# A recurrence and an MLP in one kernel: one gate tile of its own, the last token in its unit's tile, two groups of matmuls at other places

## The chip, the cores and the metric

The kernel runs on one core of a Trainium2 chip. The time is device microseconds of an execution; the number compared is the median of several executions. A profile records one execution: TensorE's matmuls (PE) and weight loads (PEld), VectorE (DVE), ScalarE (ACT), GpSimd (POOL) and the queue that issues transfers (SP). Each engine works off its own queue in order and waits on semaphores for what other engines make.

## The reference

Inputs q, k, v and f_logit have 4 batches, 8 heads, 768 tokens and 48 elements per head. A linear recurrence with a gate runs along the tokens, and its result goes through an MLP of 384 by 2048 by 384.

```python
f = 1.0 / (1.0 + np.exp(-f_logit))
for t in range(S):
    state = f[:, :, t, :, None] * state + np.einsum('bhd,bhe->bhde', k[:, :, t], v[:, :, t])
    y[:, :, t] = np.einsum('bhd,bhde->bhe', q[:, :, t], state)
x = y.transpose(0, 2, 1, 3).reshape(B * S, H * D)
h = x @ w_in
g = h * (1.0 / (1.0 + np.exp(-1.702 * h)))
return g @ w_out
```

## The kernel before

The 3072 tokens are cut into twelve units of 256 (n = 0 to 11; `NALL` is 12, `N_FILL` 3). Each unit goes through attention and then the MLP. The stored queries are shifted by one token against the other inputs, so the very last token of the whole input is left over; its y is made apart, and the last unit's tiles are 258 columns wide (`width(n)`): 256 tokens, the last token in column `U` = 256, and a column of zeros.

**Attention.** Decays are combined over levels of 1, 2, 4 to 32 tokens: `begin_gates` (L407) multiplies neighbouring gates on GpSimd (L416), first from `F`, then from level to level in the tile `tot`, of which there is one buffer for all units. The last level is the decay of a chunk of 64 tokens. For units from 5 on (`n > N_FILL + 1`) it is written to a tile of its own, `D64`, with two buffers; for the units up to 4 it lies in `tot`. `promote` (L505, L523) multiplies keys and queries with the levels on VectorE, and `set_aside` (L489) copies rows for TensorE on ScalarE (Kc L494, Qc L500). Scores are matmuls at L425, the products of keys and values at L643, y at L534 and L689. The states of a unit's four chunks are made on VectorE: a product with D64 (L667) and a sum with TensorE's result (L668), one chunk after the other. The gates of unit n + 1 are issued right after the states of unit n.

**From y to x.** ScalarE copies y out of PSUM into `yT` (L701), and `to_x` (L736) moves it to the layout that the MLP needs, `xT`, with three transfers per half of the partitions (L740 once, L745 twice). For the last unit the one token follows: 16 small matmuls (`y_last`, L724), two copies on ScalarE into a small tile `yT_last` (L730), and six transfers of its own. Then `sums_of_x` (L938) makes the sums `E` on GpSimd (L955).

**The MLP.** For units from 4 on, h is made by 20 products per unit (`mlp_h20`, L960) on sums of blocks of x (`E`) and of the weights (`WA`), and o by 7 products of eight matmul calls each (`mlp_o7`, L802), named by the PSUM tiles Y, W, X and Z that they write. Results of h are copied, added up and put through the activation by ScalarE (L1000, L1008, L1012, L1023) and VectorE (L1021) into `g`. PSUM gives h eight places, "lanes": 0 to 3 are tiles of their own, 4 and 5 are the halves of one tile (tag `y`), 6 and 7 of another (tag `sc`). `lanes["h"]` says which of the four own banks a lane takes; the four were Y, W, X and Z of the unit before.

In the last unit the columns are 258, so each product is split into two groups, and the order of the 40 products is `HALVES` (L882). An entry (x, lane) with x below 20 is product x, group 0; from 20 on product x - 20, group 1. An entry (-1, -1) puts in four of the sixteen o products of unit 10 that were held back: eight for Y, whose end (`p7`, L835) adds Y to the output on VectorE (L816), and eight for Z (`p3`, L840), with one L816. When h is done, `sum_last` (L1052) computes the last token's o on VectorE, and o of the last unit follows on TensorE.

The order of TensorE and GpSimd is the order in which the program issues (`merge` lays attention and MLP into each other); the order on VectorE, ScalarE and SP is chosen when the kernel is built, from the dependences and the order of issue.

Of the kernel before, what the change touches and what calls it, by code (L numbers as in the profile page):

```python
# [9 lines left out]
F32 = mybir.dt.float32  # L10
# [6 lines left out]
def view(t, offset, dims):  # L17

    a = t[:]
    return bass.AP(a.tensor, a.offset + offset, [list(a.ap[0])] + [list(d) for d in dims])  # L20
# [3 lines left out]
def kernel(  # L24
# [33 lines left out]
    nc = tc.nc  # L58
# [3 lines left out]
    P = 128  # L62
    C = 64
    G = 128
    U = 256
    NG = U // G
    NC = U // C
    NU = S // U
    NP = H // 2
    HS = 64  # L70
    LEV = [1 << i for i in range(C.bit_length() - 1)]
    NL = len(LEV)
    NK = DM // P
# [3 lines left out]
    N_FILL = 3  # L77
# [3 lines left out]
    NALL = B * NU  # L81
# [5 lines left out]
    att = ctx.enter_context(tc.tile_pool(name="att", bufs=1))  # L87
    wp = ctx.enter_context(tc.tile_pool(name="wp", bufs=2))
    mlp = ctx.enter_context(tc.tile_pool(name="mlp", bufs=2))
    ps = ctx.enter_context(tc.tile_pool(name="ps", bufs=1, space=bass.MemoryType.PSUM))  # L90
# [51 lines left out]
    at = [wp.tile([P, n], I32, tag="bits", name=f"at{j}", bufs=PAIRS_AHEAD) for j, n in enumerate((1, (NL - 1) * 64))]  # L142
# [16 lines left out]
    def query(n, f):  # L159

        return ((2, 3), (4, 5) if n < N_FILL else (0, 5))[n % 2][f]

    q_end = const.tile([P, NP], F32, name="q_end")
# [14 lines left out]
    for r in range(NGR):  # L178
        ffs = range(r * FG, (r + 1) * FG)
        for ff in ffs[::2]:  # L180
            f = slice(ff * P, (ff + 2) * P)
# [129 lines left out]
    def rows(h):  # L311
        return slice(h * HS, h * HS + D)
# [4 lines left out]
    last = {}  # L317

    def attention(n):
# [10 lines left out]
        t = {"tms": [F]}  # L330
        parts = []

        def part(kind):
            return lambda fn: parts.append((kind, fn))
# [72 lines left out]
        def begin_gates():  # L407
            t["tot"], off = att.tile([P, NA], F32, tag="tot", name=f"tot_{n}"), 0
            for m in LEV:
                nb = NA // (2 * m)  # L410
                t2 = t["tms"][-1].rearrange("p (n two) -> p n two", two=2)
                tn = t["tot"][:, off:off + nb]

                if m == LEV[-1] and n > N_FILL + 1:
                    tn = att.tile([P, nb], F32, tag="D64", name=f"D64_{n}", bufs=2)
                nc.gpsimd.tensor_tensor(tn, t2[:, :, 0], t2[:, :, 1], ALU.mult)  # L416
                t["tms"].append(tn)
                off += nb
# [21 lines left out]
        def columns(h, g):  # L440

            return rows(h ^ g)
# [228 lines left out]
        @part("W")  # L671
        def _():

            py = t["py"]
            for cs in ((1, 0), (2, 3)):
                for a in range(NP):
                    for c in cs:
                        g, f = CHUNK[c]  # L680
                        w = HS
                        if t["before"][c] is None:
                            if not n:
                                continue
                            w = 1
                        for h in range(2):
                            state = t["before"][c][rows(h), a] if w > 1 else t["ahead"][rows(h), NC - 1, a]
                            x = a * HALF + g * HS
                            nc.tensor.matmul(  # L689
                                py[columns(h, g), g, a, f, :w], lhsT=state, rhs=X[rows(h), query(n, f), x:x + w],  # L690
                                start=False, stop=True, skip_group_check=True,
                            )
            yT = att.tile([P, NP, NG, G], F32, tag="kn", name=f"yT_{n}", bufs=1)
            xT = mlp.tile([P, NK, width(n)], F32, tag="xT", name=f"xT_{n}", bufs=3)
            if width(n) > U:
                nc.gpsimd.memset(xT[:, :, U + 1:], 0.0)
            def half(h):
                for f in (1, 0):
                    for g in range(NG):
                        at, step = (g * HS, 1) if f else (U - 1 - g * HS, -1)  # L700
                        nc.scalar.copy(view(yT[rows(h)], at, [[U, NP], [step, HS]]), py[columns(h, g), g, :, f, :])  # L701
                to_x(lambda h: (yT[rows(h), :NK], lambda r, d: yT[r:r + d, NK]), xT[:, :, :U], NG, (h,))
            half(0)
            if n > N_FILL and n < NALL - 1:
                xTs[n] = xT

                def rest():
                    with tc.issue_after(copied["aside"].ins):
                        half(1)
                    sums_of_x(n)  # L710
                return rest
            if n == N_FILL - 1:
                xTs[n] = xT
                return lambda: half(1)
            half(1)
            xTs[n] = xT
            if n == 0:
                fetch_weights()
            if n == NALL - 1:

                pl = ps.tile([P, NP], F32, tag="sc", name="y_last")
                for a in range(NP):
                    for h in range(2):
                        nc.tensor.matmul(  # L724
                            pl[rows(h), a:a + 1], lhsT=last["st"][rows(h), NC - 1, a], rhs=q_end[rows(h), a:a + 1],
                            start=True, stop=True,
                        )
                yl = att.tile([P, NP], F32, tag="q_last", name="yT_last", bufs=1)
                for h in range(2):
                    nc.scalar.copy(yl[rows(h)], pl[rows(h)])  # L730
                yl = yl.rearrange("p (a g t) -> p a g t", g=1, t=1)
                to_x(lambda h: (yl[rows(h), :NK], lambda r, d: yl[r:r + d, NK]), xT[:, :, U:U + 1], 1)
            if n > N_FILL:
                sums_of_x(n)

        def to_x(y, x, ng, hs=range(2)):  # L736

            for h in hs:
                most, rest = y(h)
                nc.sync.dma_start(out=x[h * D:(h + 1) * D].rearrange("p c (g t) -> p c g t", g=ng), in_=most)  # L740
                at = 0
                while at < D:
                    c, p = (h * D + at) // DR, (h * D + at) % DR
                    w = min(D - at, DR - p)
                    nc.sync.dma_start(  # L745
                        out=x[D2 + p:D2 + p + w, c].rearrange("p (g t) -> p g t", g=ng), in_=rest(h * HS + at, w)
                    )
                    at += w
# [53 lines left out]
    def mlp_o7(n, g):  # L802
# [77 lines left out]
    ))  # L880

    HALVES = tuple((x % 20 if x >= 0 else None, x // 20, lane) for x, lane in (  # L882
        (38, 1), (-1, -1), (0, 6), (37, 4), (-1, -1), (-1, -1), (39, 4), (-1, -1), (34, 5), (2, 7),
        (15, 6), (30, 4), (33, 1), (22, 0), (18, 3), (1, 7), (20, 2), (25, 5), (32, 4), (24, 1),
        (6, 7), (35, 2), (13, 6), (17, 3), (21, 0), (23, 1), (16, 7), (4, 5), (7, 2), (19, 4),
        (26, 0), (27, 7), (5, 6), (14, 3), (10, 4), (9, 2), (29, 7), (3, 5), (36, 0), (31, 1),
        (12, 4), (8, 2), (28, 7), (11, 5),
# [1 line left out]
    lanes = {}  # L889
# [48 lines left out]
    def sums_of_x(n):  # L938

        w = (width(n) + 1) // 2  # L940
        room = [mlp.tile([P, NK, width(n)], F32, tag="xT", name=f"E_{n}_{i}", bufs=3).rearrange("p c t -> p (c t)")
                for i in range(2)]
        at = iter([room[i][:, j * w:(j + 1) * w] for i in range(2) for j in range(2 * NK)])
        e = E[n] = {f"b{c}{j}": xTs[n][:, c, j * w:(j + 1) * w] for c in range(NK) for j in range(2)}
        sums = [
            ("s7", "b11", "", "b21"), ("u", "b20", "", "b21"), ("z", "b01", "", "u"), ("q0", "z", "", "b00"),
            ("v", "u", "+", "b11"), ("w", "b10", "", "v"), ("t", "b01", "+", "b21"), ("x", "b00", "", "w"),
            ("q4", "q0", "+", "b10"), ("r3", "b00", "", "b10"), ("r3", "r3", "+", "b20"), ("y", "x", "", "b01"),
        ]
        if width(n) > U:  # L950
            sums = [sums[i] for i in (0, 1, 2, 3, 6, 4, 5, 8, 9, 10, 7, 11)]
        for out, x, op, y in sums:
            if out not in e:
                e[out] = next(at)
            nc.gpsimd.tensor_tensor(e[out], e[x], e[y], ALU.add if op else ALU.subtract)  # L955
# [4 lines left out]
    def mlp_h20(n, g, before):  # L960
        w = (width(n) + 1) // 2
        groups = 1 if FG * w <= 512 else 2
# [62 lines left out]
        def begin():  # L1025
            for half in range(2):
                g[half] = g_tile(f"g_{n}_{half}", width(n))
            free = lanes["o"]

            lanes["h"] = [free[x] for x in (1, 2, 0, 3)]  # L1030
            lanes["o"] = [lanes["h"][x] for x in (1, 0, 3, 2)]

        def end():
# [30 lines left out]
    xTs, halves = {}, []  # L1064

    def width(n):

        return U + 2 * (n == NALL - 1)
# [93 lines left out]


    units = [attention(n) for n in range(NALL)]
    LAG = 18 * DM

# [192 lines left out]
```

## Time and profile before

| | us |
|---|---|
| median of 5 runs | 598.95 |
| lowest, highest | 596.96, 599.67 |
| the profiled execution | 599.67 |
| its span, first to last instruction | 597.6 |
| E sums of the last unit start (L955) | 545.95 |
| last h on TensorE | 547.35 to 574.90 |
| end of the last o matmuls | 594.3 |

The mean granted clock of TensorE in that execution was 0.994. In a line of the profile in order of time stand the start and the duration in us, the engine, the line of the kernel, the operation, the tiles (output <- inputs), the shapes and how many instructions are merged; in brackets how long the engine sat idle before it and what ended that. In a table of stretches each engine has its busy time and, in brackets, its instructions.

### The profile page before, as it was taken

To read this page: it belongs to the slowest core of one execution; us is meant where nothing else is said; L and a number is where in the kernel's file an instruction comes from. 1 tells how busy PE (TensorE), PEld (TensorE's weight loads), DVE (VectorE), ACT (ScalarE), POOL (GpSimd) and SP (SyncE) were. 2 spreads that over 40 slices of the span, in tenths; PEclk is the share of its full clock that TensorE was granted. 3 is DMA by queue.
4 is the path that set the end of the run, shared out by engine and by line. 5 is a ranking of instruction groups with operands and counts; after the bars stand their busy time and mean duration, and the time that the engine had idled before them with its cause. 6 is when DMAs were issued, how large, how long until landed. Compare 5 with 4: busy or idle time off the path is not lost.

```text
span 597.6 us, 18468 instructions
## 1 busy us (share of the span) xinstructions
PE 576.0 (96%) x7814; PEld 515.0 (86%) x7814; DVE 429.8 (72%) x696; ACT 291.8 (49%) x613; POOL 136.5 (23%) x214
## 2 busy tenths in 40 slices
PE   7959899999999999999999999999999999999897
PEld 6746676867768689999999999999999999999897
DVE  2897986965766867889778789776887786361284
ACT  4745644453333352474475474574663564552440
POOL 3031110140026215420610600800700702203000
PEclk9979999999999999999999999999999999999999
DMA  7947866850143552353452343552361111001000
GB/s 181 209 105 188 197 153 190 232 118 1 38 105 79 140 124 69 74 135 88 116 149 59 78 116 88 136 134 59 93 163 44 55 45 29 27 3 26 28 1 26
DMA packets 83314, 58.29 MB, mean 98 GB/s; under 512 B 33633, under 2 KB 75265, under 8 KB 83233
## 3 DMA queue, kind: packets, MB, share of 16 engines
q1 hardware_dynamic: 82896, 56.73, 37.7%
q8 instruction: 61, 1.00, 0.7%
q10 hardware_dynamic: 337, 0.39, 0.3%
q14 instruction: 20, 0.16, 0.1%
HBM read 43.98 MB, written 8.39 MB: 88 GB/s over the span
## 4 chain that ended last, share of the span: by engine, by line
PE 87%; DVE 6%; ACT 3%; issue 2%; POOL 1%; DMA 1%; SPq 0%; DVEq 0%; ACTq 0%
PE h L993 17%; PE h L1087 13%; PE o_Y L856 11%; PE o L1101 10%; PE o_Z L856 7%; PE h_y L993 6%; PE sc L425 6%; PE o_W L856 4%; PE o_X L856 4%; PE t L357 2%; PE y L534 2%; PE y L689 2%; PE sc L643 1%; ACT yT L701 1%; DVE X L519 1%
## 5 line engine op out<-in xcount | busy, mean ns | idle before, releaser
L1087 PE MATMUL h<-xT,w_in 128*128 128x256 f32 x384 | 89.3, 389 | 2.1 <-DMA xT<-yT 2.1
L1087 PEld LDWEIGHTS h<-xT,w_in 128*128 128x128 f32 x384 | 73.1, 194 | 13.8 <-DMA xT<-yT 2.3
L523 DVE TENSOR_TENSOR X<-X,tot 128x1024 f32<-128x1024 f32 x45 | 56.9, 1264 | 38.0 <-PE sc L425 29.3
L494 ACT COPY Kc<-X 128x512 f32<-128x512 f32 x72 | 48.3, 671 | 67.1 <-DVE X L523 53.5
L1101 PE MATMUL o<-w_out,g 128*128 128x384 f32 x192 | 65.5, 492 | 0.4 <-DVE w_out L233 0.4
L955 POOL TENSOR_TENSOR E<-xT 128x128 f32<-128x128 f32 (+1 forms) x32 | 17.6, 559 | 206.7 <-DMA xT<-yT 97.2
L1101 PEld LDWEIGHTS o<-w_out,g 128*128 128x128 f32 x192 | 35.5, 190 | 22.7 <-DVE w_out L233 0.9
L993 PE MATMUL h<-E,w_in 128*128 128x128 f32 (+1 forms) x420 | 53.5, 275 | 0.0
L856 PE MATMUL o_Y<-T,S 128*128 128x192 f32 x288 | 50.7, 329 | 0.0
L993 PEld LDWEIGHTS h<-E,w_in 128*128 128x128 f32 x420 | 50.1, 192 | 0.0
L1091 ACT ACTIVATE g<-h 128x256 f32<-128x256 f32 x64 | 23.9, 383 | 49.9 <-PE h L1087 49.5
L1023 ACT ACTIVATE g<-g 128x512 f32<-128x512 f32 (+1 forms) x63 | 35.6, 582 | 25.8 <-DVE g L1021 25.4
L856 PEld LDWEIGHTS o_Y<-T,S 128*128 128x128 f32 x288 | 46.8, 190 | 0.5
L701 ACT COPY yT<-y 48x256 f32<-48x256 f32 x96 | 35.1, 366 | 21.7 <-PE y L689 20.6
L485 DVE COPY_PREDICATED A<-masks,sc 128x256 f32<-128x256 uint32 (+1 forms) x98 | 41.9, 505 | 0.1
L1021 DVE TENSOR_TENSOR g<-g,h 128x512 f32<-128x512 f32 (+1 forms) x52 | 31.7, 631 | 12.6 <-PE h L993 11.5
L372 POOL TENSOR_SCALAR F<-F 128x1024 f32<-128x1024 f32 x10 | 17.4, 1738 | 96.1 <-ACT F L375 83.3
L345 DVE STREAM_TRANSPOSE X<-raw 128x512 f32<-128x512 f32 x36 | 38.2, 1108 | 0.1
L425 PEld LDWEIGHTS sc<-X,Kc 48*64 48x64 f32 x1440 | 26.2, 136 | 11.1 <-issue 4.7
L425 PE MATMUL sc<-X,Kc 48*64 48x64 f32 x1440 | 31.0, 223 | 4.7 <-ACT Kc L494 1.7
L1021 DVE TENSOR_TENSOR g<-g,h_y 128x512 f32<-128x512 f32 (+1 forms) x26 | 16.5, 634 | 22.1 <-PE h_y L993 21.2
L1012 ACT ACTIVATE g<-h 128x512 f32<-128x512 f32 (+1 forms) x46 | 26.2, 578 | 10.3 <-PE h L993 10.0
(161 smaller groups left out, 1154.5 us busy)
## 6 DMA issues: line engine op xcount, KB each, us to landing
bits<-in_moe_w_out_dram SPq DMA_DIRECT2D x8, 768.0 KB, 7.3
raw<-in_f_logit_dram SPq DMA_DIRECT2D x48, 96.0 KB, 3.5
raw<-in_k_dram SPq DMA_DIRECT2D x48, 96.0 KB, 3.1
bits<-in_moe_w_in_dram SPq DMA_DIRECT2D x8, 576.0 KB
raw<-in_q_dram SPq DMA_DIRECT2D x44, 96.0 KB, 2.2
k_tok<-z SPq DMA_DIRECT2D x56, 64.0 KB, 1.8
kt<-k_tok SPq DMA_DIRECT2D x14, 256.0 KB, 3.1
xT<-yT SPq DMA_DIRECT2D x24, 144.0 KB, 2.7
```

What stands on the lines that cost most here:

```text
L345: nc.vector.transpose(view(out, at, [[HALF, NP], [step, R4], [R4 * step, 32]]), by_half[:, j, f].rearrange("p a (j d) -> p (a j) d", j=R4) ...
L425: nc.tensor.matmul(t["sc"][h][g * HS:(g + 1) * HS, a, s, :], lhsT=t["Kc", l][rows(h), x:x + HS], rhs=rhs(h, a, g), start=True, stop=True,)
L485: moved = nc.vector.copy_predicated(out=view(A, c * HALF + at, dims), mask=mask.bitcast(U32), data=got)
L494: nc.scalar.copy(c.rearrange("p (n two m) -> p n two m", two=2, m=m), view(X, KF * SLOT, [[2 * m, SLOT // (2 * m)], [(KR - KF) * SLOT + m, ...
L523: nc.vector.tensor_tensor(x, x, y, ALU.mult)
L701: nc.scalar.copy(view(yT[rows(h)], at, [[U, NP], [step, HS]]), py[columns(h, g), g, :, f, :])
L856: nc.tensor.matmul(t[name], lhsT=lhs(f), rhs=rhs(f), start=(new and i == 0), stop=(i == HF - 1), skip_group_check=True,)
L993: nc.tensor.matmul(ph[:, t], lhsT=WA[a][:, f * P:(f + 1) * P], rhs=E[n][b], start=(root and t == 0), stop=not goes_on, skip_group_check=True,)
L1021: nc.vector.tensor_tensor(to, to, part, ALU.add if sign > 0 else ALU.subtract)
L1023: nc.scalar.activation(to, to, AF.Gelu_apprx_sigmoid)
L1087: nc.tensor.matmul(ph, lhsT=w_in[:, c, ff * P:(ff + 1) * P], rhs=xTs[n][:, c, :], start=(c == 0), stop=(c == NK - 1))
L1101: nc.tensor.matmul(t["po"], lhsT=g[ff // FG][:, ff % FG, tt * P:(tt + 1) * P], rhs=w_out[:, ff, :], start=(ff == ffs[0]), stop=(ff == ffs[ ...
```

## The change

Three things are changed. The last level of the gates of unit 4 goes to a `D64` tile as well. The last token's y is copied into column 256 of the last unit's `yT`, which becomes 258 columns wide, and goes to `xT` with the unit's own transfers, 257 columns at a time; a function `whole` does this for the last unit. In `HALVES` two of the four groups of o are put in later, and for the last unit lanes 2 and 3 of h change their banks.

```diff
-                if m == LEV[-1] and n > N_FILL + 1:
+                if m == LEV[-1] and n > N_FILL:
                     tn = att.tile([P, nb], F32, tag="D64", name=f"D64_{n}", bufs=2)
...
+            if n == NALL - 1:
+                whole(py)
+                return
             yT = att.tile([P, NP, NG, G], F32, tag="kn", name=f"yT_{n}", bufs=1)
             xT = mlp.tile([P, NK, width(n)], F32, tag="xT", name=f"xT_{n}", bufs=3)
-            if width(n) > U:
-                nc.gpsimd.memset(xT[:, :, U + 1:], 0.0)
...
-            if n == NALL - 1:
-
-                pl = ps.tile([P, NP], F32, tag="sc", name="y_last")
-                for a in range(NP):
-                    for h in range(2):
-                        nc.tensor.matmul(
-                            pl[rows(h), a:a + 1], lhsT=last["st"][rows(h), NC - 1, a], rhs=q_end[rows(h), a:a + 1],
-                            start=True, stop=True,
-                        )
-                yl = att.tile([P, NP], F32, tag="q_last", name="yT_last", bufs=1)
-                for h in range(2):
-                    nc.scalar.copy(yl[rows(h)], pl[rows(h)])
-                yl = yl.rearrange("p (a g t) -> p a g t", g=1, t=1)
-                to_x(lambda h: (yl[rows(h), :NK], lambda r, d: yl[r:r + d, NK]), xT[:, :, U:U + 1], 1)
             if n > N_FILL:
                 sums_of_x(n)
+
+        def whole(py):
+
+            w = width(n)
+            yT = att.tile([P, NP, 1, w], F32, tag="kn", name=f"yT_{n}", bufs=1)
+            xT = mlp.tile([P, NK, w], F32, tag="xT", name=f"xT_{n}", bufs=3)
+            nc.gpsimd.memset(xT[:, :, U + 1:], 0.0)
+            pl = ps.tile([P, NP], F32, tag="sc", name="y_last")
+            for a in range(NP):
+                for h in range(2):
+                    nc.tensor.matmul(
+                        pl[rows(h), a:a + 1], lhsT=last["st"][rows(h), NC - 1, a], rhs=q_end[rows(h), a:a + 1],
+                        start=True, stop=True,
+                    )
+            for h in range(2):
+                for f in (1, 0):
+                    for g in range(NG):
+                        at, step = (g * HS, 1) if f else (U - 1 - g * HS, -1)
+                        nc.scalar.copy(view(yT[rows(h)], at, [[w, NP], [step, HS]]), py[columns(h, g), g, :, f, :])
+                nc.scalar.copy(yT[rows(h), :, 0, U], pl[rows(h)])
+                to_x(
+                    lambda h: (yT[rows(h), :NK, :, :U + 1], lambda r, d: yT[r:r + d, NK, :, :U + 1]), xT[:, :, :U + 1], 1, (h,)
+                )
+            xTs[n] = xT
+            sums_of_x(n)
...
     HALVES = tuple((x % 20 if x >= 0 else None, x // 20, lane) for x, lane in (
-        (38, 1), (-1, -1), (0, 6), (37, 4), (-1, -1), (-1, -1), (39, 4), (-1, -1), (34, 5), (2, 7),
-        (15, 6), (30, 4), (33, 1), (22, 0), (18, 3), (1, 7), (20, 2), (25, 5), (32, 4), (24, 1),
+        (38, 1), (-1, -1), (0, 6), (37, 4), (-1, -1), (39, 4), (34, 5), (2, 7), (-1, -1),
+        (15, 6), (30, 4), (33, 1), (22, 0), (18, 3), (-1, -1), (1, 7), (20, 2), (25, 5), (32, 4), (24, 1),
...
-            lanes["h"] = [free[x] for x in (1, 2, 0, 3)]
+            lanes["h"] = [free[x] for x in ((1, 2, 0, 3) if groups == 1 else (1, 2, 3, 0))]
             lanes["o"] = [lanes["h"][x] for x in (1, 0, 3, 2)]
```

## The prediction, made before the changed kernel ran

> **What bounds the kernel now.** I read the page's busy times and chain first, then busy time by stretch, then the order of time around the two places that the diff touches.
>
> ```profile
> span 597.6 us, 18468 instructions
> ...
> PE 576.0 (96%) x7814; PEld 515.0 (86%) x7814; DVE 429.8 (72%) x696; ACT 291.8 (49%) x613; POOL 136.5 (23%) x214
> ```
>
> ```profile
> core 0: us, PE busy (x) PEld busy (x) DVE busy (x) ACT busy (x) POOL busy (x), PEclk, DMA share, GB/s
> 226.00:246.00 20.00, 19.25 (x404) 18.20 (x403) 15.72 (x25) 6.63 (x18) 9.15 (x10) 1.00 0.26 58
> 530.00:547.35 17.35, 17.13 (x292) 16.59 (x291) 8.59 (x17) 6.25 (x17) 1.25 (x3) 1.00 0.13 25
> 547.35:574.90 27.55, 24.98 (x194) 23.64 (x193) 9.68 (x24) 11.87 (x32) 3.69 (x9) 1.00 0.05 16
> ```
>
> TensorE is the bound: 96% busy, and the chain that ends last lies on it for 87% of the span. The change removes no matmul, so it can only take away TensorE's waits. The stretches show how much there is: from 226 to 246 us (unit 4 hands over to unit 5) the weight loads leave 1.80 us free, switches between kinds of matmul included; in the last h (547.35 to 574.90) they leave 3.91 us; in the 17.35 us before it only 0.76. From 260 to 530 PE is busy 270.0 of 270 us. These are the places to read in order of time.
>
> First, unit 5's gates:
>
> ```profile
> 231.19 1.75 DVE L795 TENSOR_TENSOR S<-g 128x512 f32<-128x512 f32 x1
> ...
> 235.73 1.04 POOL L416 TENSOR_TENSOR tot<-F 128x512 f32<-128x512 f32 x1 [3.32 <-DVE st L667]
> ...
> 236.18 0.70 PE L425 MATMUL sc<-Qc,Kc 48*64 48x64 f32 x32 [0.22 <-DVE st L668]
> ...
> 239.28 0.36 DVE L667 TENSOR_TENSOR st<-st,D 128x192 f32<-128x192 f32 x1 [1.97 <-POOL D L416]
> 239.56 1.22 DVE L523 TENSOR_TENSOR X<-X,tot 128x1024 f32<-128x1024 f32 x1
> ...
> 244.54 0.59 PEld L425 LDWEIGHTS sc<-Qc,Kc 48*64 48x64 f32 x32 [0.80 <-ACT Kc L494]
> ```
>
> GpSimd waits 3.32 us until unit 4's last state product (L667) has read its decay out of `tot`; VectorE then waits 1.97 us for the new decay D, with the promote (L523) queued behind it; at the end of that chain TensorE waits 0.80 us for Kc.
>
> Second, the last h:
>
> ```profile
> 545.95 0.78 POOL L955 TENSOR_TENSOR E<-xT 128x129 f32<-128x129 f32 x2 [17.14 <-DMA xT<-yT_last]
> ...
> 547.35 0.58 PEld L993 LDWEIGHTS h<-E,N_c 128*128 128x128 f32 x4
> ...
> 552.59 0.58 PEld L993 LDWEIGHTS h_y<-E,w_in 128*128 128x128 f32 x4
> ...
> 553.44 0.39 ACT L1012 ACTIVATE g<-h_y 128x258 f32<-128x258 f32 x1 [2.68 <-PE h_y L993]
> ...
> 554.70 0.35 DVE L816 TENSOR_TENSOR osb<-osb,o_Z 128x192 f32<-128x192 f32 x1 [2.37 <-PE o_Z L856]
> ...
> 556.03 0.52 PEld L993 LDWEIGHTS h_sc<-xT,N_p 128*128 128x128 f32 x4 [0.67 <-ACT g L1012]
> ...
> 558.97 0.52 PEld L993 LDWEIGHTS h_sc<-E,w_in 128*128 128x128 f32 x4 [0.64 <-ACT h_sc L1000]
> ...
> 561.12 0.52 PEld L993 LDWEIGHTS h_y<-xT,N_p 128*128 128x128 f32 x4 [0.73 <-ACT g L1008]
> ```
>
> The row at 545.95 says that the E sums wait for the last token's transfers. But the h that uses them starts at 547.35 without a wait: the o matmuls before it last until then. The three waits below have one form: a product writes one half of a shared PSUM tile (h_sc is lanes 6 and 7, h_y is 4 and 5) and waits until ScalarE has read the other half. Counting entries of the order: 556.03 is product (15, 6) after (2, 7), 558.97 is (1, 7) after the copy into lane 6 of what (18, 3) made, 561.12 is (32, 4) after (25, 5).
>
> **Part 1, gates apart.** One tile more is taken from D64 (it has two buffers), no instruction is added. Removed is the wait of unit 5's gates for unit 4's states. The gates can't start at once: ahead of them in GpSimd's queue lie the sums in place (L917), which end at 229.46 + 2.94 = 232.40. So they start 3.3 us sooner, and D is there about 3 us sooner if nothing else slows it. VectorE's 1.97 us go, the promote starts up to 2.0 us earlier, and TensorE's 0.80 us vanish; the other free time there is switching. Gain at most 0.8.
>
> Against it: the gates now run beside unit 4's state chain on VectorE (233.36 to 236.03: four L668, three L667 between), which they followed before. L795 shows what meeting GpSimd costs: 1.75 us beside L917, against 1.28 for two, 0.64 each, at 537.43 with GpSimd idle. It was held about 1.1 us, until GpSimd's instruction ended. The gates of unit 5 last 1.05, 0.95, 0.41, 0.30, 0.25 and 0.23 us in the chain of waits. By the same pattern the first L667 meets the rest of the first gate (0.15), the next the rest of the second (0.4), the third a short one (0.2): some 0.6 us in all, where the lower end is 0. TensorE's L425 at 236.18 already waits 0.22 us for the last L668, so this delay falls on it in full. I take +0.6 - 0.8 = **-0.2 us**. Ends: -0.8 with no collision; and if L795 and the three L667 each wait for a whole gate, 1.05 + 0.95 + 0.41 + 0.30 = 2.7 - 0.8 = +1.9.
>
> The Trainium skill (SBUF — State Buffer, "SBUF: two separate sides") speaks against this part: VectorE with two SBUF inputs and GpSimd exclude each other for a whole instruction. L795's 1.75 us agree with it. It would make L667 wait and leave L668, with one operand in PSUM, alone; a rule of no exclusion would give -0.8 for the part instead of -0.2.
>
> **Part 2, last token.** Removed: six DMA issues on SP (one of 0.64 and two of 0.62 us per half, 540.73 to 544.66). Moved: the 16 small matmuls stay where they are on TensorE (between L689 and o_Y); the two small copies on ScalarE (0.155 us each) now follow each half's four copies. The first half's transfers start 0.16 later, about 536.87, the second's at about 538.87, ending on SP near 540.8. The last issue before began at 544.04 (half of the two from 543.43) and POOL started at 545.95, 1.9 later; so E starts near 542.1 to 542.6, some 3.4 us earlier. Rows of 1028 bytes instead of 1024 are not in the trace; a landing twice as long (3.8 us) still gives 544.5. Worth **0 us**: TensorE's o matmuls cover E until 547.35. The copy of o_Y (L820, 538.54) comes behind the same ten ScalarE copies as before, and its reader starts at 539.55. Ends: 0 and 0, as both covers exceed 0.7 us.
>
> **Part 3, groups and lanes.** A group is four o products, 1.25 us (550.04 to 551.29 in the trace). Before, four groups follow entries 38, 37 (two) and 39; now they follow 38, 37, (2, 7) and (18, 3). I set the new order out with the trace's steps (0.44 us per product, 0.05 at a switch):
> - to 551.29 nothing changes; 39 starts at 551.34 instead of 552.59.
> - (34, 5) now follows 39 (lane 4) directly. From 39's start to the end of its eviction was 553.44 + 0.39 - 552.59 = 1.24 us, so 34 starts at 552.63: a new wait of 0.8.
> - (2, 7) 553.07, group 553.55 to 554.80, (15, 6) at 554.85: its wait of 0.67 is covered.
> - 30, 33, 22, (18, 3) at 556.63, group 557.12 to 558.37, (1, 7) at 558.42: its wait of 0.64 is covered.
> - (20, 2) would start at 558.86. Lane 2 is now Z's bank, free when L816 has read Z: 0.71 after the group's end (554.34 to 555.05 in the trace), 559.08. It starts at 559.13, a new wait of 0.27, against 559.41 before.
>
> Behind that the order is the old one, so the rest moves with it: **-0.3 us**. Ends: -1.3 if neither new wait appears (0.67 + 0.64); +0.5 if L816 stands behind one more VectorE pass and its hand-over (1.0 instead of 0.27: -1.31 + 0.8 + 1.0). The stretch from 574.90 moves along; the last token's sums end at 588.65 on VectorE, 2.0 us before TensorE asks for them.
>
> **Sum.** -0.2 + 0 - 0.3 = -0.5 us. The profiled execution took 599.67 (span 597.6, 2.1 around it), so it would take 599.2. The median shown is 598.95, 0.7 below the profiled one; on it the forecast is 598.45.
>
> **Rivals.**
> - *Both pairs of waits really go*: no collision on VectorE and no new wait in the last h, -0.8 - 1.3 = -2.1, 596.85. For: VectorE's L667 last 0.36 us and may fall into gaps between gates. Against: three waits of the same form in this very stage. The five runs also lie in two clumps, near 597.0 and from 598.95 to 599.67, so a small real gain with the median in the lower clump reads the same.
> - *A wait takes the place of the one removed (slower)*: at the hand-over from 232.4 us, the gates hold up L795 and each L667, 2.7 us, less 0.8. It decides from 0.8 us of delay on: above that part 1 is a loss. Full price +1.9, with part 3's -0.3 it is +1.6, 600.55; without part 3's gain 600.85. For: L795's own 1.75. Against: gates shrink quickly, the fourth lasts 0.30.
> - *The transfers set the last h*, and part 2 is a gain by itself: the page's 17.14 us of waiting speaks for it; the start at 547.35 without a wait against it. With no TensorE time to win before 547.35 this ends at the forecast.
>
> **How the numbers follow.** A measurement here tells about 0.3%, 1.8 us, from no change. The forecast (small sums of either sign, and the third rival with it) has 0.44, the first rival 0.38, the second 0.18. So faster 0.38, same 0.44, slower 0.18, and the time is the likeliest case's, 598.4 (its own range 597.2 to 599.6). The first rival's end with the lower clump, 597.0 - 0.8, gives the low bound 596.2; the second's 600.55 the high one, 600.5.
>
> **What would show it.** Part 1: L416 of unit 5 near 232.4 to 233 instead of 235.73, no wait for D on L667, the three L667 stretched from 0.36, and L425 at 244.54 without its wait. Part 2: E sums from about 542.5, h still at 547.35 after the shift. Part 3: no waits at (15, 6) and (1, 7), new ones of 0.8 at (34, 5) and 0.3 at (20, 2). I am wrong if h needs E earlier than its own start, if lanes 4 and 5 don't hold each other up, or if ScalarE or VectorE come in another order elsewhere and TensorE waits between 260 and 530 us.

## The result, and the profile after

The changed kernel took 597.94 us in the median (595.64 to 600.94, 34 runs), the kernel before 599.06 (596.96 to 600.87, 58 runs, those shown above among them). The ratio is 0.9984, with a 95% interval of 0.9976 to 0.9992: 0.16%, about 1.0 us faster (0.5 to 1.4), which is a gain, but a smaller one than the 0.3% that the prediction takes as the least that a measurement here tells from no change.

The profiled executions differ by more: 597.64 against 599.67 us, spans of 595.5 and 597.6. Of these 2.0 us, 0.93 were there already when the first of unit 4's o matmuls started (224.91 against 225.84 us), before anything that the change touches. Over all profiled executions of this study that point lay between 224.1 and 226.1 us, changed or not, so the opening (all that runs before that point) scatters by some 2 us. The comparison that counts is therefore made between two points of TensorE's own order. The table of stretches after, for the hand-over from unit 4 to unit 5 and for the last h:

```profile
core 0: us, PE busy (x) PEld busy (x) DVE busy (x) ACT busy (x) POOL busy (x), PEclk, DMA share, GB/s
224.91:243.10 18.19, 17.91 (x338) 16.96 (x337) 15.12 (x24) 6.57 (x17) 9.33 (x10) 1.00 0.29 65
...
545.83:572.98 27.15, 24.97 (x193) 23.64 (x193) 9.68 (x24) 11.86 (x32) 0.96 (x3) 1.00 0.05 16
```

The hand-over, from the first o_Y of unit 4 to the second scores of unit 5, is 18.19 us long; before it ran from 225.84 to 244.54, 18.70: 0.51 us gone. The last h is 27.15 us long against 27.55: 0.40 us gone, with the same weight loads (23.64 us busy in both), so waits alone went. TensorE's granted clock is 1.00 in these stretches before and after, so the clock is not what differs. Between the two stretches lie 302.73 us against 302.81; in the nine profiled executions of this study that length runs from 302.73 to 302.82, so these 0.08 us are scatter. The two stretches give 0.91 us, and the ratio says 0.96.

The hand-over in order of time, after the change:

```profile
230.26 1.75 DVE L808 TENSOR_TENSOR S<-g 128x512 f32<-128x512 f32 x1
231.43 1.49 POOL L416 TENSOR_TENSOR tot<-F 128x512 f32<-128x512 f32 x1
...
232.79 0.36 DVE L667 TENSOR_TENSOR st<-st,D 128x192 f32<-128x192 f32 x1
232.99 1.89 POOL L416 TENSOR_TENSOR tot<-tot 128x256 f32<-128x256 f32 x4
...
233.57 0.36 DVE L667 TENSOR_TENSOR st<-st,D 128x192 f32<-128x192 f32 x1
...
234.35 0.42 DVE L667 TENSOR_TENSOR st<-st,D 128x192 f32<-128x192 f32 x1
...
234.96 0.21 POOL L416 TENSOR_TENSOR D<-tot 128x16 f32<-128x16 f32 x1
...
235.28 0.59 PEld L425 LDWEIGHTS sc<-Qc,Kc 48*64 48x64 f32 x32 [0.41 <-PE y L689]
...
236.54 1.23 DVE L523 TENSOR_TENSOR X<-X,tot 128x1024 f32<-128x1024 f32 x1 [0.51 <-PE sc L425]
...
243.10 0.56 PEld L425 LDWEIGHTS sc<-Qc,Kc 48*64 48x64 f32 x32 [0.22 <-issue]
```

GpSimd's first gate now starts at 231.43, behind its sums of weights, and waits for no state. It lasts 1.49 us instead of 1.04 because it meets VectorE's L808 (line 795 before), which lasts until 232.01. The three state products beside the gates last 0.36, 0.36 and 0.42 us, so they are hardly held up, and TensorE asks for the first scores 10.37 us into the stretch instead of 10.31. The promote starts at 236.54, 11.63 us into the stretch instead of 13.72, and before the second scores TensorE waits for nothing but the switch of 0.22 us, where it had 0.80. The decay D is there at 235.17, 10.26 us into the stretch.

Two of the gates after the change, by themselves:

```profile
232.99 0.63 POOL L416 TENSOR_TENSOR tot<-tot 128x256 f32<-128x256 f32 x1
...
234.27 0.29 POOL L416 TENSOR_TENSOR tot<-tot 128x64 f32<-128x64 f32 x1
```

And before the change D, 13.41 us into the stretch when it is done, with the row of VectorE that ran beside the first two gates:

```profile
235.95 1.36 DVE L800 TENSOR_TENSOR g<-g,S 128x512 f32<-128x512 f32 x1
...
239.03 0.22 POOL L416 TENSOR_TENSOR D<-tot 128x16 f32<-128x16 f32 x1
```

The last h in order of time, after the change:

```profile
540.99 1.33 POOL L968 TENSOR_TENSOR E<-xT 128x129 f32<-128x129 f32 x2 [13.69 <-PE o_X L869]
...
545.83 0.58 PEld L1006 LDWEIGHTS h<-E,N_c 128*128 128x128 f32 x4
...
551.06 0.52 PEld L1006 LDWEIGHTS h_y<-xT,w_in 128*128 128x128 f32 x4 [0.71 <-ACT g L1025]
...
553.20 0.58 PEld L1006 LDWEIGHTS h_sc<-xT,N_p 128*128 128x128 f32 x4
...
556.73 0.58 PEld L1006 LDWEIGHTS h_sc<-E,w_in 128*128 128x128 f32 x4
557.50 0.52 PEld L1006 LDWEIGHTS h<-E,N_c 128*128 128x128 f32 x4 [0.19 <-DVE osb L829]
...
559.19 0.52 PEld L1006 LDWEIGHTS h_y<-xT,N_p 128*128 128x128 f32 x4 [0.73 <-ACT g L1021]
...
567.27 0.52 PEld L1006 LDWEIGHTS h_sc<-xT,w_in 128*128 128x128 f32 x4 [1.05 <-DVE g L1034]
```

E starts 4.84 us ahead of h instead of 1.40, and h starts where the o matmuls before it end, as it did. The row of E names o_X, whose matmuls end at 540.95; with the token alone (below) E starts just as long after y, 12.14 us against 12.20 here, and the row names the transfers, so they most likely end this wait too. (15, 6) at 553.20 and (1, 7) at 556.73 have no wait any more; (34, 5) at 551.06 has a new one of 0.71 us, and (20, 2) at 557.50 one of 0.19, for the read of Z. The wait of (32, 4) stands as it was. So does the longest one, 1.05 us of (5, 6) at 567.27: there the other half of the tile is read by VectorE, not by ScalarE. In all, the weight loads leave 3.51 us of this stretch free (27.15 less 23.64), and all but the 0.19 are waits for the other half of a shared tile.

### The profile page after: what moved, and what is told of

It reads as the page before. It is cut to its first block, busy times and chain, and to the rows that moved or that the text cites. A ratio compares the mean times of both kernels' runs of the same rounds, so it can differ in the third digit from the quotient of the medians.

```text
span 595.5 us, 18457 instructions
## 1 busy us (share of the span) xinstructions
PE 575.9 (97%) x7814; PEld 514.2 (86%) x7814; DVE 429.0 (72%) x696; ACT 291.8 (49%) x613; POOL 138.7 (23%) x214
## 4 chain that ended last, share of the span: by engine, by line
PE 87%; DVE 7%; ACT 3%; issue 1%; DMA 1%; POOL 1%; SPq 0%; DVEq 0%; ACTq 0%
PE h L1006 17%; PE h L1100 13%; PE o_Y L869 11%; PE o L1114 10%; PE o_Z L869 8%; PE h_y L1006 6%; PE sc L425 6%; PE o_X L869 4%; PE o_W L869 4%; PE y L689 2%; PE t L357 2%; PE y L534 2%; PE sc L643 1%; DVE X L519 1%; ACT yT L703 1%
## 5 line engine op out<-in xcount | busy, mean ns | idle before, releaser
L1100 PE MATMUL h<-xT,w_in 128*128 128x256 f32 x384 | 90.5, 391 | 1.9 <-DMA xT<-yT 1.9
L703 ACT COPY yT<-y 48x256 f32<-48x256 f32 x88 | 32.2, 366 | 17.9 <-PE y L689 16.7
```

The lines of the kernel that those rows point to most:

```text
L1100: nc.tensor.matmul(ph, lhsT=w_in[:, c, ff * P:(ff + 1) * P], rhs=xTs[n][:, c, :], start=(c == 0), stop=(c == NK - 1))
```

## The experiments

All edits are against the kernel before or the changed kernel, as said. The stretches are those of the section above.

### One part at a time

Three kernels make one part of the change each, on the kernel before. The gates:

```diff
-                if m == LEV[-1] and n > N_FILL + 1:
+                if m == LEV[-1] and n > N_FILL:
```

> Part 1 by itself on the kernel before. Theory (the parts are independent; unit 4 to 5 pays): TensorE's stretch from the o_Y that starts unit 4's last MLP part (225.84 before) to the second score matmuls of unit 5 (244.54) shrinks from 18.70 to 18.2 us, L667 stay near 0.36 us, the last h keeps its 27.55 us; ratio 0.9991. Rival (the gain needs the other parts, or was the opening's scatter): stretch 18.7, ratio 1.000. Rival (port collisions cost): L667 stretched and stretch 18.5 or more.

The last token (the function `whole` and what it replaces, with the old order of groups and the old lanes):

```diff
+            if n == NALL - 1:
+                whole(py)
+                return
...
```

> Part 2 by itself. Theory (the transfers were covered): E sums start some 3.5 us earlier against the last h, h starts without a wait as before, the last h keeps 27.55 us; ratio 1.000. Rival (the transfers set the last h): the stretch from y (L534 at 530.31 before) to the end of h, 44.6 us, shrinks by 0.5 us or more.

The groups and lanes:

```diff
-        (38, 1), (-1, -1), (0, 6), (37, 4), (-1, -1), (-1, -1), (39, 4), (-1, -1), (34, 5), (2, 7),
-        (15, 6), (30, 4), (33, 1), (22, 0), (18, 3), (1, 7), (20, 2), (25, 5), (32, 4), (24, 1),
+        (38, 1), (-1, -1), (0, 6), (37, 4), (-1, -1), (39, 4), (34, 5), (2, 7), (-1, -1),
+        (15, 6), (30, 4), (33, 1), (22, 0), (18, 3), (-1, -1), (1, 7), (20, 2), (25, 5), (32, 4), (24, 1),
...
-            lanes["h"] = [free[x] for x in (1, 2, 0, 3)]
+            lanes["h"] = [free[x] for x in ((1, 2, 0, 3) if groups == 1 else (1, 2, 3, 0))]
```

> Part 3 by itself, with the last token's transfers as before. Theory: the last h goes from 27.55 to 27.15 us, with a wait of 0.7 at (34, 5) and none at (15, 6) and (1, 7); E is early enough also without part 2; ratio 0.9993. Rival (part 3 needs the earlier E of part 2): new waits of TensorE on E at (39, 4) to (2, 7), last h 27.5 us or more, ratio 1.000 or above.

| kernel | hand-over, us | last h, us | ratio to before |
|---|---|---|---|
| before | 18.70 | 27.55 | 1 |
| gates alone | 18.19 | 27.54 | 0.9988 (0.9975 to 1.0001) |
| last token alone | 18.68 | 27.55 | 0.9992 (0.9978 to 1.0006) |
| groups and lanes alone | 18.68 | 27.15 | 0.9993 (0.9978 to 1.0007) |
| the whole change | 18.19 | 27.15 | 0.9984 (0.9976 to 0.9992) |

The ratios of the single parts can't be told from 1, nor from each other; the stretches can. Each gain belongs to its own part and is there in full without the others: 0.51 us for the gates, 0.40 for the groups, nothing for the token (from y to the end of the last h 44.58 us, 44.59 before). The new places of the groups and the new banks of lanes 2 and 3 were not run apart. With the token alone E starts 4.9 us ahead of h:

```profile
542.29 1.23 POOL L968 TENSOR_TENSOR E<-xT 128x129 f32<-128x129 f32 x2 [13.63 <-DMA xT<-yT]
...
547.19 0.58 PEld L1006 LDWEIGHTS h<-E,N_c 128*128 128x128 f32 x4
```

Yet h starts with the end of the o matmuls and is as long as before. With the groups alone, E at its old time, no product of h waits for E either: the rival that part 3 needs part 2 falls too.

### The gates issued twice

Was the low price of the collision on VectorE a property of the state products, or their luck?

```diff
-                nc.gpsimd.tensor_tensor(tn, t2[:, :, 0], t2[:, :, 1], ALU.mult)
+                for _ in range(2 if n == N_FILL + 2 else 1):
+                    nc.gpsimd.tensor_tensor(tn, t2[:, :, 0], t2[:, :, 1], ALU.mult)
```

> The changed kernel with each of unit 5's gate products issued twice on GpSimd (the same result written twice), so that all of unit 4's state chain on VectorE runs beside GpSimd. Theory (a product whose second operand repeats one element is not held up by GpSimd): the three L667 stay at 0.36 to 0.42 us, the state chain at 2.75 us from the first L668 to the end of the last. Rival (they exclude each other, and in the changed kernel the products fell between GpSimd's instructions by luck): at least one L667 at 0.7 us or more, the chain 3.3 us or longer.

One execution. VectorE in order of time (the edit moves the lines by one, so the products are L668 and the sums L669 here), then two of GpSimd's gates that it meets:

```profile
233.60 0.34 DVE L669 TENSOR_TENSOR st<-st,sc 128x192 f32<-128x192 f32 x1
...
233.98 0.36 DVE L668 TENSOR_TENSOR st<-st,D 128x192 f32<-128x192 f32 x1
...
234.75 0.69 DVE L668 TENSOR_TENSOR st<-st,D 128x192 f32<-128x192 f32 x1
...
235.87 0.36 DVE L668 TENSOR_TENSOR st<-st,D 128x192 f32<-128x192 f32 x1
```

```profile
234.17 1.06 POOL L417 TENSOR_TENSOR tot<-F 128x512 f32<-128x512 f32 x1
...
235.31 0.61 POOL L417 TENSOR_TENSOR tot<-tot 128x256 f32<-128x256 f32 x1
```

The second product begins at 234.75, in the middle of a gate that ends at 235.23, and itself ends at 235.44, 0.33 us late. The others met no long remainder: the first begins 0.12 us before the end of its gate (232.61 to 234.10), and the gate at 235.31 ends at 235.92, 0.05 after the third begins. The sum at 233.60 ran wholly beside the gate that ends at 234.10 and took its usual 0.34 us: it has one operand in PSUM, and the prediction expected it to be left alone. The chain from the first sum to the end of the last takes 3.01 us (233.60 to 236.61). Neither expectation is met in full, 0.69 and 3.01 against 0.7 and 3.3, but the theory that such products are never held up has fallen: one was, until GpSimd's instruction ended. In the changed kernel the products start near the ends of gates. The first gate there ends at 232.92 and the second, of 0.63 us, at 233.62, and the products begin at 232.79 and 233.57. The third begins at 234.35, 0.21 us before the fourth gate's end at 234.56, and is the one that takes 0.42 us. Both products that were held end 0.21 us after the gate (235.44 and 234.77), so about 0.15 of their 0.36 us had passed beside it. That is an estimate from two rows; it fits the four products that began with 0.05 to 0.13 us of a gate left and lost nothing.

The hand-over took 19.16 us here: D came at 239.96, its reader on VectorE waited 2.74 us, and TensorE's wait before the second scores was back:

```profile
239.99 0.36 DVE L668 TENSOR_TENSOR st<-st,D 128x192 f32<-128x192 f32 x1 [2.74 <-POOL D L417]
```

```profile
245.24 0.59 PEld L426 LDWEIGHTS sc<-Qc,Kc 48*64 48x64 f32 x32 [0.92 <-ACT Kc L495]
```

With D 10.26, 13.41 and 13.87 us into the stretch (changed kernel, kernel before, gates twice) the idle time before the second scores is 0.22, 0.80 and 0.92 us. So it is the time of D, and the promote behind it, that decides this wait. The state chain's delay reaches TensorE in full, as the prediction said: the chain is 0.34 us longer than before (3.01 against 2.67), and the first scores are asked for 10.64 us into the stretch instead of 10.31.

### Two products between 39 and 34

Of the two lines of the order, only the entries from (39, 4) to (18, 3) are shown.

```diff
-(39, 4), (34, 5), (2, 7), (-1, -1),
-(15, 6), (30, 4), (33, 1), (22, 0), (18, 3),
+(39, 4), (2, 7), (22, 0), (34, 5), (-1, -1),
+(15, 6), (30, 4), (33, 1), (18, 3),
```

> The changed kernel with (2, 7) and (22, 0) put between (39, 4) and (34, 5) in the order of the last h; nothing else. Theory (lanes 4 and 5 hold each other up until ScalarE has read, and another lane's products cover it): the wait of 0.71 us at (34, 5) goes, the last h shrinks from 27.15 to 26.4 us, ratio to before 0.997. Rival (the wait has another cause, or moves on to the next product): last h 27.0 us or more, ratio 0.998.

TensorE's weight loads in order of time, from (39, 4) to (34, 5):

```profile
550.73 0.58 PEld L1002 LDWEIGHTS h_y<-E,w_in 128*128 128x128 f32 x4
551.23 0.53 PEld L1002 LDWEIGHTS h_sc<-E,w_in 128*128 128x128 f32 x4
551.67 0.53 PEld L1002 LDWEIGHTS h<-E,w_in 128*128 128x128 f32 x4
552.12 0.53 PEld L1002 LDWEIGHTS h_y<-xT,w_in 128*128 128x128 f32 x4
```

The stretch of the last h:

```profile
546.79:573.15 26.36, 24.71 (x193) 23.56 (x193) 9.67 (x24) 11.87 (x32) 0.95 (x3) 1.00 0.05 16
```

(34, 5) starts 1.39 us after (39, 4), with two products done in between and no wait; in the changed kernel it was 1.29 with nothing in between. The last h is 26.36 us long, 0.79 less, of which that wait is 0.71; the other waits stand as they were. The ratio to the kernel before is 0.9969 (0.9953 to 0.9984).

### All of the last h in such an order

```python
(38, 1), (-1, -1), (0, 6), (37, 4), (-1, -1), (39, 4), (2, 7), (22, 0), (34, 5), (-1, -1), (15, 6), (30, 4),
(33, 1), (18, 3), (-1, -1), (1, 7), (25, 5), (20, 2), (24, 1), (32, 4), (6, 7), (35, 2), (21, 0), (13, 6),
(17, 3), (23, 1), (16, 7), (4, 5), (7, 2), (26, 0), (19, 4), (27, 7), (14, 3), (9, 2), (10, 4), (5, 6),
(36, 0), (3, 5), (31, 1), (29, 7), (12, 4), (8, 2), (28, 7), (11, 5),
```

> The changed kernel with the products of the last h so ordered that between two products on lanes 4 and 5, or 6 and 7, there stand two or three on other lanes. Theory (all waits in the last h have this form): last h at 23.2 to 24.5 us instead of 27.15, TensorE's waits there under 1 us, ratio to before 0.992 to 0.994. Rival (VectorE and ScalarE set the pace once TensorE waits less): h shortens by under 1.5 us, or the o matmuls after it wait for the sums of g and take back what h gained; ratio 0.996 or above.

The stretches of its last h and of what follows it:

```profile
545.11:568.70 23.59, 23.59 (x193) 23.38 (x193) 9.82 (x24) 11.82 (x32) 0.96 (x3) 1.00 0.05 18
568.70:591.20 22.50, 19.41 (x117) 18.24 (x115) 13.94 (x27) 3.81 (x11) 0.00 (x0) 1.00 0.05 18
```

The last h takes 23.59 us, 3.56 less than in the changed kernel, where 3.51 us were free, and TensorE is busy in all of it. So the waits on the shared tiles went, those with VectorE as the reader too, and the 0.19 with them. The stretch behind is 22.50 us, as in the changed kernel (572.98 to 595.5, 22.5), so nothing is taken back: VectorE and ScalarE keep up, with 9.82 and 11.82 us of work. It took 593.56 us in the median of 6 runs; the ratio to the kernel before is 0.9907 (0.9882 to 0.9932). The two stretches account for 0.51 + 3.96 = 4.5 us, 0.9925, inside the interval. This version beats both kernels: all its 6 runs (592.61 to 596.81 us) lie below the lowest of 10 runs of the changed kernel taken beside it (597.07).

### The changed kernel again, beside the two orders

> The changed kernel again, beside the two orders on the same chip: ratio to before 0.9984, last h 27.15 us.

Ratio 0.9979 (0.9963 to 0.9995), hand-over 18.19 us, last h 27.15.

## Why the prediction was right

The time lay within the range and near the forecast: 597.94 us against 598.4. That alone proves little, for the range is 4.3 us wide and an unchanged kernel would have lain in it as well. The forecast of the change was half of what came: -0.5 us against -0.91 in the two stretches. The parts of the sum show where the rest lies.

- **The bound.** TensorE's waits were all there was to win: busy weight loads in the last h are the same to 0.01 us in both kernels.
- **Part 1** was forecast at -0.2 and measured at -0.51. The mechanism was right: D came 3.15 us earlier in the stretch and the promote 2.09, where about 3 and up to 2.0 were forecast. Two terms of its sum were mis-sized. The wait that vanishes was put at 0.80 us, but 0.22 of that was the switch, which stays: 0.58 went. The collision was put at 0.6 (its three terms, 0.15, 0.4 and 0.2, add up to 0.75) and measured 0.06. What was left of the gates when the products began was 0.13, 0.05 and 0.21 us, so only the second was far off; but the price is less than what is left, by about 0.15. The lengths of the gates were taken where the gates themselves were held up: the second was 0.95 us long before, in the time of VectorE's L800 (1.36 us from 235.95), and 0.63 in the changed kernel. That the products began so near the gates' ends was luck; the gates twice show that the cost is there where they don't.
- **Part 2** was forecast at 0 with E 3.4 us sooner. Against the start of h it is 3.44 sooner, and the part alone leaves the last h at 27.55 us. The third rival is right about the 17 us of waiting and wrong about what it is worth.
- **Part 3** was forecast at -0.3 (the order set out entry by entry, 559.13 against 559.41; its terms are -1.31, +0.8 and +0.27) and measured at -0.40: the old waits of 0.67 and 0.64 went, the new ones are 0.71 and 0.19. The steps from entry to entry hold to 0.1 us.
- **The first rival** (both pairs of waits go) had the right form for the gates and the wrong one for the groups. The wait of lane 5 for lane 4 came as forecast, and both reorderings show that it is this wait and not the count of groups that held the last h back. **The slower rival** has its mechanism, seen at 0.06 us in the changed kernel and at 0.33 with the gates twice, and not its size.

What remains open: why two lanes in one PSUM tile wait for each other. The profile puts these waits down to semaphores, so they are in the program; whether two tiles of one bank each would do without it wasn't tried. The Trainium skill (PSUM — Partial Sum Buffer, "PSUM bank collisions raise a hardware error") says that two engines on different banks run clean. No run here shows it for the two halves of one tile.

## What to carry to other kernels

A long wait of an engine beside the bound (17 us for E) is worth nothing where the bound engine has work until the result is there; look for the bound engine's own waits in one stage and ask what form they share. Here a tile that two products use in turn made each wait for the other's reader, and filling the gaps with products on other tiles brought 3.56 us, where the whole change brought about 0.9. Where an opening scatters by more than the effect, compare stretches between two points of the bound engine's order; the scatter drops out, and parts of 0.4 us can be told apart.

## What was not expected of the hardware

VectorE waits for the end of GpSimd's instruction also when its second operand repeats each of its elements 48 times (the state product, 0.36 us alone, 0.69 when it began 0.48 us before a gate's end, 0.42 when it began 0.21 before one). The sum with one operand in PSUM does not (0.34 us inside a gate). The price depends on where they meet: three products beside the gates cost 0.06 us in all, for about the first 0.15 us of a product passed beside a gate. A row's length taken from a place where the two engines meet is not the length elsewhere: the same gate took 0.95 us beside one of VectorE's dense sums and 0.63 beside the state products.
